# First half of the modulation's weights in four loads of every fourth partition, 48 KB a row

## Chip, cores, metric

One core of one Trainium2 chip. The metric is the device time of one execution in microseconds; lower is better.

Terms: SP is the engine whose queue issues nearly all loads here. A load is dealt to 16 DMA engines; each of its rows (the bytes that go to one partition) is one packet of the trace. PE is the matmul engine, DVE the vector engine; PE's granted clock is the share of its full clock that the chip let it have. "Stride" below means the step over partitions.

## The reference, cut to what matters

A decode step of a transformer block for 8 sequences: a modulation computed from `c`, attention over an 8192-long cache, and a gated MLP.

```python
mod = (_silu(c) @ w_mod).reshape(c.shape[0], 6, 1, -1)     # w_mod: 1024 x 6144, bf16
sa, ca, ga, sb, cb, gb = ...                               # six parts of mod
h = _layernorm(x) * (1 + ca) + sa
x = x + ga * attention(h, k_cache, v_cache, wq, wo)        # caches: 134 MB
h = _layernorm(x) * (1 + cb) + sb
return x + gb * mlp(h, W_gate, W_up, W_down)
```

`w_mod` is 12.6 MB, the first thing that is loaded and the first weights that are used. All inputs together are 185.6 MB.

## The kernel before: the parts that matter

`arena` is a buffer of 128 partitions. `load` queues a load, `pump` issues queued loads in order as soon as nothing unread lies where they go. Each partition gets 8 rows of `w_mod`, 96 KB; the first four (24 * D elements, 48 KB) are the first half.

```python
        def load(key, src, n, lo):
            place[key] = lo
            stream.append((key, src, n, lo))
        # ... pump(): dst = arena[:, lo:lo + n]; P.op("sp", ... e.dma_start(dst, src) ...)
        wm_src = w_mod.rearrange("(p k) n -> p (k n)", k=KC)
        # ... cut
        load(("wm", 0), wm_src[:, 0:D], D, 0)                      # 2 KB a row
        load(("wm0", 0), wm_src[:, D:24 * D], 23 * D, D)           # 46 KB a row
        load(("wm", 1), wm_src[:, 24 * D:48 * D], 24 * D, 24 * D)  # 48 KB a row: the second half
        # ... wq, then k, k, v for each of 8 sequences, wo, W_gate, W_up, W_down
        head = stream[2:]
        del stream[2:]
        pump()
        # ... c and A_x: two loads of 32 rows of 512 B, issued on ACT's queue
        stream.extend(head)
        # ... the matmuls of the modulation (line 522), in two halves:
        for i in range(2):
            # ... 48 matmuls
            P.op("pe", fns, reads=[R("hT"), slot_r(place["wm", i], place["wm", i] + 24 * D)], writes=[bank(0, 3)])
        # ... at the end of the program
        start_loads_first(nc, 3)     # moves SP's first 3 loads ahead of the start barrier's wait
```

The small first load was there so that the engines would have something to do early.

Of the kernel before, what the change touches and what calls it, by code (L numbers as in the profile page):

```python
# [236 lines left out]
def start_loads_first(nc, n):  # L237

    block = nc.main_func.blocks[0]

    def where(ins, engine, opcode=None):
        return [i for i, x in enumerate(ins) if x.engine == engine and opcode in (None, x.opcode)]

    for engine, ahead, total in ((mybir.EngineType.SP, 2, n), (mybir.EngineType.Activation, 2, 2)):
        ins = list(block.instructions)
        at = where(ins, engine, "EventSemaphore")[0]
        first = [ins[i] for i in where(ins, engine) if i > at][:total]
        assert all(x.opcode == "DMACopy" and not x.sync_info.on_wait for x in first), [x.opcode for x in first]
        names = {x.name for x in first}
        rest = [x for x in ins if x.name not in names]  # L250
        at = where(rest, engine, "EventSemaphore")[0]
        rest = rest[:at] + first[ahead:] + rest[at:]
        at = where(rest, engine)[0]
        block.instructions = rest[:at] + first[:ahead] + rest[at:]


def hold_weights(nc, held):

    names = {x.ins.name for x in held}
    for block in nc.main_func.blocks:  # L260
        block.instructions = [copy.replace(x, ldweights=False) if x.name in names else x for x in list(block.instructions)]


def bass_adaLN_cond__gqa_block_cached__glu_gated_reglu__decode_kernel(nc, A_x, A_k_cache, A_v_cache, A_wq, A_wo, B_x, B_W_gate, B_W_up, B_W_down, c, w_mod, out):
    B, _, D = A_x.shape
# [27 lines left out]
    with ExitStack() as es:  # L293
        E = es.enter_context

        def sb(name, shape, dtype):
            return E(nc.sbuf_tensor(name, shape, dtype))
# [4 lines left out]
        arena = sb("arena", [128, RING], dt.bfloat16)  # L302
# [74 lines left out]
        def slot_r(lo, hi):  # L377
            return ("arena", lo, hi)
# [2 lines left out]

        stream, place = [], {}

        def load(key, src, n, lo):
            place[key] = lo
            stream.append((key, src, n, lo))

        def pump():
            while stream:
                key, src, n, lo = stream[0]  # L390
                if P.unread("arena", lo, lo + n):
                    return
                stream.pop(0)
                dst = arena[:, lo:lo + n]
                P.op("sp", lambda e, dst=dst, src=src: e.dma_start(dst, src), writes=[slot_r(lo, lo + n)], dma=True,  # L395
                     own=key[0] if key[0] in ("ka", "kb", "v") else None)
                if key[0] in ("ka", "kb", "v"):
                    P.held[key] = (lo, lo + n)

        wm_src = w_mod.rearrange("(p k) n -> p (k n)", k=KC)  # L400
# [2 lines left out]
        g_src = B_W_gate.rearrange("(p k) n -> p (k n)", k=KC)  # L403
        u_src = B_W_up.rearrange("(p k) n -> p (k n)", k=KC)
        d_src = B_W_down.rearrange("(p k) n -> p (k n)", k=KF)
        load(("wm", 0), wm_src[:, 0:D], D, 0)
        load(("wm0", 0), wm_src[:, D:24 * D], 23 * D, D)
        load(("wm", 1), wm_src[:, 24 * D:48 * D], 24 * D, 24 * D)
        wq_parts = [(0, 4), (4, 8)]
        for i, (r0, r1) in enumerate(wq_parts):  # L410
# [9 lines left out]
        wd_parts = [(0, 14), (14, 21), (21, 25), (25, 27), (27, 28)]  # L420
        for i, (r0, r1) in enumerate(wd_parts):
            load(("wd", i), d_src[:, r0 * D:r1 * D], (r1 - r0) * D, VPART + r0 * D)
        head = stream[2:]
        del stream[2:]
        pump()
        for t, src in enumerate((c.rearrange("b (j n) -> (b j) n", j=4), A_x.rearrange("b o (j n) -> (b o j) n", j=4))):
            P.op("act", lambda e, t=t, src=src: e.dma_start(cx[:, t, :], src), writes=[R("cx", t, t + 1)], dma=True)
        stream.extend(head)
        P.pump = pump
        pump()  # L430


# [106 lines left out]
        for i, (r0, r1) in enumerate(wq_parts):  # L539
            lo, hi = place["wq", i], place["wq", i] + (r1 - r0) * 4096  # L540
# [11 lines left out]
        for z in range(2):  # L552
            src = ps[:, 4 + z, :].rearrange("p (u x r) -> p u r x", u=J, r=2)
            dst = qs[:, 16 * z:16 * z + 16, :].rearrange("p (u r) x -> p u r x", r=2)
# [146 lines left out]
        for z in range(2):  # L701
# [6 lines left out]
            dst = orow[:, 4 * z:4 * z + 4, :].rearrange("p j d -> p (j d)")  # L708
# [46 lines left out]
        for nm, b0 in (("gate", 0), ("up", 2)):  # L755
            lo, hi = place[nm, 0], place[nm, 0] + KC * F
# [18 lines left out]
        for i, (r0, r1) in enumerate(wd_parts):  # L775
            lo, hi = place["wd", i], place["wd", i] + (r1 - r0) * D
# [35 lines left out]

        P.plan()
        P.emit(nc, dict(sp=nc.sync, act=nc.scalar, pool=nc.gpsimd, dve=nc.vector, pe=nc.tensor), sems)
        start_loads_first(nc, 3)
        hold_weights(nc, holding)


# [26 lines left out]
```

## Time and profile before

| | |
|---|---|
| time, three runs | 436.29 us median (436.08 to 436.56) |
| bytes moved | 185.74 MB in a span of 434.9 us |
| busy: load queue, PE, DVE | 99.0%, 60%, 57% |

The page of the profile. "DMA" gives the busy share of the 16 DMA engines in 40 slices of the span (9 is 90% or more), "GB/s" counts a packet in the slice in which it starts, and the last lines are the chain of work that ended last.

```profile
span 434.9 us, 4853 instructions
...
DMA  9999999989999999999999999999999999999996
GB/s 374 452 431 434 433 434 437 471 375 440 440 413 428 455 440 407 434 455 413 431 464 422 416 434 464 410 425 443 458 398 431 443 464 410 448 429 429 427 418 255
DMA packets 5526, 185.74 MB, mean 427 GB/s; under 512 B 720, under 2 KB 784, under 8 KB 1168
...
q1 hardware_dynamic: 5376, 185.61, 99.0%
...
## 4 chain that ended last, share of the span: by engine, by line
DMA 11%; PE 4%; DVE 1%; SPq 0%; issue 0%
```

The engines that move data are hardly idle between the first slice and the last, and no other engine is near that. Time can be gained only where the DMA engines run below their usual rate, and that is at the start. The timeline of the first 36 us: start, duration, engine, line, operation, and in brackets the idle time before it and what ended it.

```profile
0.00 1.44 SPq L395 DMA_DIRECT2D arena<-in_w_mod_dram  x3
...
1.42 0.20 POOL L437 MEMSET identf<- 128x128 f32 x1 [0.98 <-POOLq L830]
1.57 22.18 SPq L395 DMA_DIRECT2D arena<-in_A_wq_dram  x2
...
9.78 0.58 PE L455 MATMUL ps<-cx,rsel 32*128 32x512 bf16 x1 [9.78 <-DMA cx<-in_A_x_dram]
...
19.23 4.16 PE L522 MATMUL ps<-arena,hT 128*32 128x512 bf16 x48
...
31.54 4.82 PE L522 MATMUL ps<-arena,hT 128*32 128x512 bf16 x48 [8.15 <-DMA arena<-in_w_mod_dram]
```

PE has the first half's matmuls done at 23.4 us and then waits 8.15 us for the second half's bytes. The issue of loads, with KB and the time from issue to landing:

```profile
arena<-in_w_mod_dram SPq DMA_DIRECT2D x1, 6144.0 KB, 30.4
arena<-in_w_mod_dram SPq DMA_DIRECT2D x1, 5888.0 KB, 16.5
arena<-in_w_mod_dram SPq DMA_DIRECT2D x1, 256.0 KB, 2.8
```

Below, "packet records" are the trace's list of packets: start, duration and size of each, without the engine or the partition. Time is counted from the start of SP's first issue.

### The profile page before, as it was taken

What the parts mean: (1) busy time and instruction counts of PE and PEld (TensorE: products, weight loads), DVE (VectorE), ACT (ScalarE), POOL (GpSimd) and SP (SyncE); (2) the same over time, 40 slices, a digit from 0 to 9 for tenths busy, and PEclk for the clock granted to TensorE, in tenths of its full rate; (3) what the DMA queues carried; (4) which work ended last, traced back from release to release, by engine and by line L of the source; (5) the groups of instructions that cost most, each with busy time, mean ns of one, the idle gap of its engine ahead of it and who ended that gap; (6) DMA issues with size and microseconds to landing.
All of it is one profiled execution on the core that took longest, in us unless ns stands there. A gap on an engine that the chain in (4) does not pass through costs nothing. (4 is left out here: it accounts for less than half of the span.)

```text
span 434.9 us, 4853 instructions
## 1 busy us (share of the span) xinstructions
PE 260.7 (60%) x2175; PEld 137.3 (32%) x2015; DVE 249.8 (57%) x345; ACT 29.8 (7%) x55; POOL 9.2 (2%) x24
## 2 busy tenths in 40 slices
PE   0325339566838874783977478487838856364247
PEld 0100003163218224421822352172226316241015
DVE  0603059747972985597299649739963974430021
ACT  1100010100020002002000200200020020100000
POOL 3000000000000000000000000000000000000000
PEclk9966569969978996998699599979968986885678
DMA  9999999989999999999999999999999999999996
GB/s 374 452 431 434 433 434 437 471 375 440 440 413 428 455 440 407 434 455 413 431 464 422 416 434 464 410 425 443 458 398 431 443 464 410 448 429 429 427 418 255
DMA packets 5526, 185.74 MB, mean 427 GB/s; under 512 B 720, under 2 KB 784, under 8 KB 1168
## 3 DMA queue, kind: packets, MB, share of 16 engines
q1 hardware_dynamic: 5376, 185.61, 99.0%
q8 instruction: 5, 0.08, 0.1%
q10 hardware_dynamic: 144, 0.04, 0.0%
q14 instruction: 1, 0.01, 0.0%
HBM read 185.63 MB, written 0.02 MB: 427 GB/s over the span
## 5 line engine op out<-in xcount | busy, mean ns | idle before, releaser
L584 DVE STREAM_TRANSPOSE kt<-arena 128x1024 uint32<-128x1024 uint32 x128 | 148.2, 1211 | 62.1 <-DVEq L181 44.7
L594 PE MATMUL ps<-kt,qpad 128*128 128x512 bf16 x512 | 133.9, 384 | 42.8 <-DVE kt L584 36.7
L634 PE MATMUL ps<-arena,pT 128*64 128x256 bf16 x1024 | 74.8, 321 | 51.0 <-PEq L181 51.0
L634 PEld LDWEIGHTS ps<-arena,pT 128*64 128x64 bf16 x1024 | 72.0, 132 | 53.2 <-issue 52.3
L594 PEld LDWEIGHTS ps<-kt,qpad 128*128 128x128 bf16 x512 | 40.5, 98 | 132.3 <-DVE kt L584 99.7
L624 DVE TENSOR_SCALAR pT<-pd,mqf 128x1024 bf16<-128x1024 bf16 x64 | 28.2, 503 | 0.6
L616 ACT ACTIVATE prb<-ps,bias 128x1024 bf16<-128x1024 f32 x16 | 17.7, 1110 | 138.8 <-DVE mjt L611 138.8
L622 DVE STREAM_TRANSPOSE pd<-prb 128x1024 bf16<-128x1024 bf16 x16 | 19.8, 1238 | 10.9 <-ACT prb L616 10.9
L600 DVE TENSOR_REDUCE negm<-ps 128x1 f32<-128x512 f32 x32 | 21.2, 661 | 4.5 <-PE ps L594 4.5
L762 PE MATMUL ps<-arena,hT 128*32 128x448 bf16 x128 | 10.7, 518 | 16.9 <-DMA arena<-in_B_W_up_dram 10.6
L769 DVE TENSOR_TENSOR kt<-ps,kt 128x448 bf16<-128x448 f32 x2 | 1.2, 620 | 27.8 <-PE ps L762 27.8
L546 PE MATMUL ps<-arena,hT 128*32 128x512 bf16 x64 | 7.2, 630 | 12.2 <-DMA arena<-in_A_wq_dram 12.2
L522 PE MATMUL ps<-arena,hT 128*32 128x512 bf16 x96 | 9.0, 551 | 8.2 <-DMA arena<-in_w_mod_dram 8.2
L653 ACT ACTIVATE oacc<-ps 128x32 f32 (+1 forms) x9 | 1.8, 198 | 158.6 <-PE ps L648 158.6
L575 POOL TENSOR_TENSOR qpad<-qR,mq 128x128 bf16<-128x128 bf16 x8 | 4.9, 607 | 310.7 <-DVE pT L624 258.2
L529 DVE COPY mod<-ps 128x512 f32<-128x512 f32 x2 | 1.3, 671 | 16.5 <-PE ps L522 16.5
L762 PEld LDWEIGHTS ps<-arena,hT 128*32 128x32 bf16 x64 | 2.3, 134 | 25.1 <-DMA arena<-in_B_W_up_dram 11.7
L557 DVE CAST kt<-ps 128x512 bf16<-128x512 f32 x1 | 0.7, 692 | 15.9 <-PE ps L546 15.9
L783 PE MATMUL ps<-arena,hmT 128*32 128x256 bf16 x84 | 6.4, 329 | 3.9 <-DMA arena<-in_B_W_down_dram 3.9
L606 PE MATMUL ps<-identf,negm 128*128 128x128 f32 x16 | 3.9, 326 | 7.8 <-DVE negm L604 7.8
L722 PE MATMUL ps<-arena,kt 128*32 128x256 bf16 x128 | 4.9, 328 | 4.6 <-DMA arena<-in_A_wo_dram 4.6
L546 PEld LDWEIGHTS ps<-arena,hT 128*32 128x32 bf16 x32 | 1.2, 137 | 18.2 <-DMA arena<-in_A_wq_dram 14.8
(99 smaller groups left out, 88.9 us busy)
## 6 DMA issues: line engine op xcount, KB each, us to landing
arena<-in_A_k_cache_dram SPq DMA_DIRECT2D x16, 4096.0 KB, 27.2
arena<-in_A_wq_dram SPq DMA_DIRECT2D x2, 4096.0 KB, 34.2
arena<-in_B_W_gate_dram SPq DMA_DIRECT2D x1, 7168.0 KB, 24.2
arena<-in_B_W_up_dram SPq DMA_DIRECT2D x1, 7168.0 KB, 28.8
arena<-in_w_mod_dram SPq DMA_DIRECT2D x1, 6144.0 KB, 30.4
arena<-in_w_mod_dram SPq DMA_DIRECT2D x1, 5888.0 KB, 16.5
arena<-in_B_W_down_dram SPq DMA_DIRECT2D x1, 3584.0 KB, 19.0
arena<-in_B_W_down_dram SPq DMA_DIRECT2D x1, 1792.0 KB, 22.9
```

The source lines that it names most:

```text
L522: fns.append(lambda e, w=w, pr=pr, j=j, kk=kk: hold(e.matmul(ps[32 * j:32 * j + 32, pr, :], hT[:, kk, :], w[:, 2 * pr:2 * pr + 2, j, :], s ...
L546: fns.append(lambda e, w=w, r=kk - r0, z=z, g=g, kk=kk: hold(e.matmul(ps[32 * g:32 * g + 32, 4 + z, :], hT[:, kk, :], w[:, r, g, z, :], st ...
L575: P.op("pool", lambda e: e.tensor_tensor(out=qpad[:, :, 24:152].rearrange("p u (q c) -> p u q c", q=4)[:, :, :, 0:J], in0=qR[:].rearrange( ...
L584: P.op("dve", lambda e_: e_.transpose(ktb[:, to:to + PART].bitcast(dt.uint32), arena[:, lo:lo + PART].bitcast(dt.uint32)), reads=[slot_r(l ...
L594: fns.append(lambda e_, t=t, r=r: e_.matmul(ps[:, e // 4, :].rearrange("p (c k) -> p c k", k=32), qpad[:, t * 2 + r, 24 - 8 * i:152 - 8 * ...
L600: P.op("dve", lambda e: e.tensor_reduce(negm[:, h:h + 1], ps[:, h, :], AX.X, ALU.max, negate=True), reads=[bank(h)] + (free(("ka", b)) if ...
L616: P.op("act", lambda e: e.activation(prb[:, f, :], ps[:, 2 * f:2 * f + 2, :].rearrange("p h n -> p (h n)"), ACT.Exp, bias=bias[:, 0:1], sc ...
L622: P.op("dve", lambda e: e.transpose(pd[:, f], prb[:, f]), reads=[R("prb", f, f + 1)], writes=[R("pd", 1024 * f, 1024 * f + 1024)])
L624: P.op("dve", lambda e, g=g: e.tensor_scalar(out=pT[:, f, :, :, g, :], in0=pd[:, f].rearrange("p (c i x) -> p c i x", c=32, i=2), scalar1= ...
L634: fns.append(lambda e, n=n, h=h, c_=c_, i=i, t=t: e.matmul(ps[64 * t:64 * t + 64, 5, 0:2 * Dh].rearrange("p (i d) -> p i d", d=Dh), pT[:, ...
L762: fns.append(lambda e, w=w, kk=kk, h=h, j=j, b0=b0: hold(e.matmul(ps[32 * j:32 * j + 32, b0 + h, 0:H], hT[:, kk, :], w[:, kk, j, h, :], st ...
L783: fns.append(lambda e, w=w, r=k - r0, k=k, i2=i2, j=j: e.matmul(ps[32 * j:32 * j + 32, 4, 0:256], hmT[:, k, 1 - i2:33 - i2], w[:, r, i2, j ...
```

## The change

Its intent: no small rows, full-length rows from the first microsecond. The first half comes in four loads, each of every fourth partition, so each load has 32 rows of 48 KB, two for each engine. Why not 32 neighbouring partitions? Because those lie on half of SBUF's ports.

```diff
-        def load(key, src, n, lo):
+        def load(key, src, n, lo, dst=None):
             place[key] = lo
-            stream.append((key, src, n, lo))
+            stream.append((key, src, n, lo, arena[:, lo:lo + n] if dst is None else dst))
@@ pump() takes dst from the queue: cut @@
-        load(("wm", 0), wm_src[:, 0:D], D, 0)
-        load(("wm0", 0), wm_src[:, D:24 * D], 23 * D, D)
+        place["wm", 0] = 0
+        for i in range(4):
+            load(("wm0", i), wm_src[i::4, 0:24 * D], 6 * D, 6 * D * i, arena[i:128:4, 0:24 * D])
         load(("wm", 1), wm_src[:, 24 * D:48 * D], 24 * D, 24 * D)
@@ cut @@
-        head = stream[2:]
-        del stream[2:]
+        head = stream[4:]
+        del stream[4:]
@@ cut @@
-        start_loads_first(nc, 3)
+        start_loads_first(nc, 5)
```

More of the change, by code (lines that the diff above doesn't have):

```diff
@@ L382, in bass_adaLN_cond__gqa_block_cached__glu_gated_reglu__decode_kernel @@
         stream, place = [], {}
-        def load(key, src, n, lo):
+        def load(key, src, n, lo, dst=None):
             place[key] = lo
-            stream.append((key, src, n, lo))
+            stream.append((key, src, n, lo, arena[:, lo:lo + n] if dst is None else dst))
         def pump():
             while stream:
-                key, src, n, lo = stream[0]
+                key, src, n, lo, dst = stream[0]
                 if P.unread("arena", lo, lo + n):
@@ L393, in pump @@
                 stream.pop(0)
-                dst = arena[:, lo:lo + n]
                 P.op("sp", lambda e, dst=dst, src=src: e.dma_start(dst, src), writes=[slot_r(lo, lo + n)], dma=True,
```

## The prediction

> **What bounds the kernel now.** The DMA engines. The page's 40 slices show them at nine tenths or more nearly throughout; the queue table gives the load queue 99.0% of 16 engines' span, 427 GB/s over 434.9 us. The chain of waits ends with the loads of W_gate and W_down and 4 us of arithmetic behind the last bytes. PE is busy 60%, DVE 57%: neither sets the time. The change can only give what it takes out of slow DMA time.
>
> **Where the start loses time.** In the trace's packet records (time from the first load's issue) the first 2 KB row starts at 1.01 us, and all 16 engines have started by 1.39. Each moves eight 2 KB rows (84 ns at best, up to 556 here) and starts its first 46 KB row between 1.77 and 2.46 us. From 1 to 2 us the engines move 229 GB/s, from 2 to 4 us 384, afterwards 430 to 434: about 0.7 us lost. A 46 KB row takes 1740 ns, a 48 KB row 1815, both 27 B/ns.
>
> **The change.** It removes 128 rows of 2 KB and 128 of 46 KB, and adds four loads of 32 rows of 48 KB: two rows an engine and load. Bytes are the same. Packets should fall from 5526 to about 5430, those under 8 KB from 1168 to about 1072.
>
> *Gain.* An engine's 48 KB rows should begin where its 2 KB rows began, 1.01 to 1.39 us, and take 8 x 1.815 = 14.5 us, plus up to 0.45 us for a slow first row (some first 46 KB rows took 2.19 us) and 0.15 for small packets. The second half of the weights, which now starts at 16.2 to 16.7 us, should start near 15.8 to 16.3: a gain of 0.3 to 0.6 us. Since DMA is the limit to the end, it arrives there whole.
>
> *Off the path.* SP issues two loads more before the start barrier, 0.33 to 0.42 us each: POOL's memset of identf moves from 1.42 to about 2.1 us. The small loads of c and x slip between whole rows; with no 2 KB rows ahead, the first small matmul (L455, 9.75 us) starts near 12 to 13 us, the first modulation matmul (L522) near 22 instead of 19.2. It takes 4.2 us and must end before the second half lands, near 31: it will.
>
> **The risk.** The Trainium skill, "DMA: Bandwidth & Descriptors", section "The descriptor swizzle", says that a load of 128 partitions gives each engine the eight partitions of one SBUF port; the trace agrees in so far as all 16 run at full rate side by side. The section covers that shape only. With every fourth partition each port holds two of the 32 rows, but if rows are dealt to engines in plain order, two engines write one port at a time. The first 6.3 MB would then run at half rate: rows near 3.6 us, the second half starting near 29 us, the end 13 us later, near 449. I give this about one chance in five; nothing in the trace of before decides it.
>
> **Prediction.** 436.0 us; range 435.2 to 449.0, wide because of the second case. Faster by over 2%: 0.01; within 2%: 0.78; slower: 0.21.
>
> **What would show it.** Right: 48 KB packets of about 1.8 us from the first microsecond on, second half near 16 us, later GB/s and tail unchanged. Wrong: first rows well over 2 us, GB/s near 220 in the first 30 us, PE's wait at L522 13 us later. Also wrong if a late x (after 20 us) made the first modulation matmul the limit, or if later loads were issued so late that the queue ran dry.

## More of the kernel before

Executions come in two states. Most of this kernel's take 436 to 437 us; some take 444 to 446 us, of the kernel before as well as of changed ones.

## The result, and the profile after

| | before | after |
|---|---|---|
| median of 6 runs, us | 436.30 (435.88 to 444.27) | 436.91 (436.34 to 445.25) |
| ratio of fast runs | 1 | 1.0012, 95% interval 0.9999 to 1.0026 |

A ratio is the mean time of one kernel's fast runs over the mean of the other's of the same rounds, so it is not quite the ratio of the medians.

The profiled run of the changed kernel fell into the slow state (445.25 us). These are its stretches, with busy time of PE, PEld, DVE, ACT and POOL, then PE's granted clock, DMA share and GB/s:

```profile
0.00:8.00 8.00, 0.00 (x0) 0.00 (x0) 0.00 (x0) 1.28 (x1) 4.29 (x16) 1.00 0.99 390
8.00:80.00 72.00, 27.43 (x201) 7.24 (x105) 22.53 (x40) 4.58 (x7) 0.46 (x1) 0.72 1.00 387
90.00:160.00 70.00, 47.49 (x375) 28.00 (x372) 47.68 (x66) 5.00 (x10) 1.27 (x2) 0.88 1.01 435
```

From 8 to 80 us the engines are as busy as ever but move 387 GB/s instead of 435. The kernel before has such runs too (444 to 445 us), so this is no effect of the change, and this profile is not used further. The profile after, from here on, is that of the same kernel run again (run `after_again`). Its page, the lines that answer to those shown of before:

```profile
span 435.3 us, 4856 instructions
...
DMA  9999999999999999999999999999999999999995
GB/s 364 434 449 434 432 434 440 464 393 467 413 422 434 470 410 422 434 470 394 434 449 458 394 431 452 428 425 461 422 425 434 473 404 464 392 423 444 435 407 242
DMA packets 5430, 185.74 MB, mean 427 GB/s; under 512 B 752, under 2 KB 816, under 8 KB 1072
...
q1 hardware_dynamic: 5280, 185.61, 98.8%
...
## 4 chain that ended last, share of the span: by engine, by line
DMA 13%; DVE 5%; PE 5%; issue 0%; DVEq 0%
```

The packet counts are those predicted (5430, and 1072 under 8 KB). The busy share is no better. The timeline:

```profile
0.00 3.41 SPq L394 DMA_DIRECT2D arena<-in_w_mod_dram  x5
...
1.85 0.20 POOL L437 MEMSET identf<- 128x128 f32 x1 [1.42 <-POOLq L830]
3.55 22.07 SPq L394 DMA_DIRECT2D arena<-in_A_wq_dram  x2
...
10.72 0.58 PE L455 MATMUL ps<-cx,rsel 32*128 32x512 bf16 x1 [10.72 <-DMA cx<-in_A_x_dram]
...
20.17 5.08 PE L522 MATMUL ps<-arena,hT 128*32 128x512 bf16 x48
...
32.16 4.21 PE L522 MATMUL ps<-arena,hT 128*32 128x512 bf16 x48 [6.92 <-DMA arena<-in_w_mod_dram]
```

The second half's matmuls, which wait for bytes in both kernels, start at 32.16 us instead of 31.54 (31.66 in two more profiles of before, 32.31 in another of the change). The change made the start of the stream later, not earlier. And SP took 3.41 us for five issues where it took 1.44 for three. The four loads land 11.1 us after their issue (median):

```profile
arena<-in_w_mod_dram SPq DMA_DIRECT2D x4, 1536.0 KB, 11.1
arena<-in_w_mod_dram SPq DMA_DIRECT2D x1, 6144.0 KB, 29.3
```

In the packet records, rows after an engine's first take 1815 ns in the median, the full rate. So the case that the prediction feared, two engines on one port, did not come about. But the first row starts at 1.32 us instead of 1.01, and the 16 first rows take 2.38 to 2.83 us, 2.54 on average.

Theories for the lost time:

1. Loads at a stride of four partitions are issued and dealt out later.
2. Long first rows start slowly, whatever load they belong to: either because the issue of the following loads gets in their way (2a), or by themselves (2b).
3. The number of issues in the first 3 us slows the start.

### The profile page after: what moved, and what is told of

It reads as the page before. It is cut to its first block, busy times and chain, and to the rows that moved or that the text cites. A ratio compares the mean times of both kernels' runs of the same rounds, so it can differ in the third digit from the quotient of the medians.

```text
span 443.9 us, 4856 instructions
## 1 busy us (share of the span) xinstructions
PE 264.6 (60%) x2175; PEld 139.7 (31%) x2015; DVE 249.7 (56%) x345; ACT 29.8 (7%) x55; POOL 9.2 (2%) x24
## 2 busy tenths in 40 slices
DMA packets 5430, 185.74 MB, mean 418 GB/s; under 512 B 752, under 2 KB 816, under 8 KB 1072
## 5 line engine op out<-in xcount | busy, mean ns | idle before, releaser
L762 PE MATMUL ps<-arena,hT 128*32 128x448 bf16 x128 | 12.1, 572 | 14.5 <-DMA arena<-in_B_W_up_dram 10.9
L722 PE MATMUL ps<-arena,kt 128*32 128x256 bf16 x128 | 6.4, 393 | 4.8 <-DMA arena<-in_A_wo_dram 4.8
L546 PEld LDWEIGHTS ps<-arena,hT 128*32 128x32 bf16 x32 | 1.2, 137 | 20.8 <-DMA arena<-in_A_wq_dram 17.4
```

Of the source, the lines that this page charges most:

```text
L546: fns.append(lambda e, w=w, r=kk - r0, z=z, g=g, kk=kk: hold(e.matmul(ps[32 * g:32 * g + 32, 4 + z, :], hT[:, kk, :], w[:, r, g, z, :], st ...
L722: fns.append(lambda e, w=w, k=k, j=j: e.matmul(ps[32 * j:32 * j + 32, 5, 0:256], oX[:, k, :], w[:, k, j, :], start=(k == 0), stop=(k == KO ...
L762: fns.append(lambda e, w=w, kk=kk, h=h, j=j, b0=b0: hold(e.matmul(ps[32 * j:32 * j + 32, b0 + h, 0:H], hT[:, kk, :], w[:, kk, j, h, :], st ...
```

## Experiments

Two measures are used. The first is the ratio of times; it resolves about 0.13%, 0.6 us. The second is read from the packet records and resolves more: the time by which 6.3 MB have been moved (the first half of the weights), and its parts. A packet's bytes are spread evenly over its duration for this. "Idle" is the time in the first 8 us in which an engine has no packet in flight, the mean of 16 engines. "Excess" is what the packets that start in the first 6 us take beyond the usual time of their size (1815 ns for 48 KB, 1740 for 46 KB, 84 for 2 KB; between sizes seen later, interpolated), over 16.

| run | SP's first issue, us | first row starts, us | idle, us | excess, us | 6.3 MB moved, us |
|---|---|---|---|---|---|
| before (three profiles) | 0.39 | 1.01, 1.01, 1.02 | 1.15, 1.16, 1.07 | 0.50, 0.54, 0.70 | 16.33, 16.36, 16.43 |
| the change (two fast profiles) | 0.54, 0.55 | 1.32, 1.33 | 1.42, 1.43 | 0.74, 0.84 | 16.75, 16.86 |
| one_long | 0.39 | 1.01 | 1.29 | 0.61 | 16.53 |
| four_cols | 0.39 | 1.01 | 1.15 | 0.64 | 16.52 |
| two_strided | 0.55 | 1.32 | 1.54 | 0.66 | 16.78 |
| small_then_strided | 0.39 | 1.02 | 1.23 | 0.74 | 16.65 |
| first_8k | 0.39 | 1.01 | 1.11 | 0.63 | 16.45 |
| first_512b | 0.39 | 1.02 | 1.43 | 0.90 | 17.09 |
| four_blocks | 0.39 | 1.01 | 1.17 | 3.86 | 31.50 |

Three profiles of before differ by 0.10 us in the last column, two of the change by 0.11; a difference of 0.1 between single profiles says nothing. All kernels gave correct results. Diffs are against the changed kernel unless said otherwise; the number in `stream[...]` and in `start_loads_first` follows the number of loads and is left out.

### after_again: the change once more

No edit.

> The changed kernel again, for a profile in the fast state. Both theories: 436.5 to 437.0 us. Theory 1 (loads of 32 rows at a stride are issued and dealt out later) and theory 2 (long first rows start slowly whatever the load's shape) both expect the profile to repeat what the slow one had in its first 4 us: SP takes 0.47 to 0.59 us for each of the four issues (0.33 to 0.42 before), the first row starts near 1.3 us and the last engine's near 2.4 us, first rows take 2.2 to 2.8 us, later rows 1.815; second half of the weights starts at 16.8 to 17.4 us (16.2 to 16.7 before).

Measured: ratio 1.0002 (0.9987 to 1.0017), median 436.77 us over all six runs, two of them slow. SP's issues of the four loads took 0.47 to 0.59 us, the first row started at 1.32 us, the last of the engines' first rows at 1.73 (not 2.4), first rows took 2.38 to 2.83 us, and the second half started at 16.6 to 17.3 us. The start is as in the slow profile, but for the last engine. In time the loss does not stand out from the noise: 1.0012, 1.0002.

### one_long: long rows without the stride

```diff
-        for i in range(4):
-            load(("wm0", i), wm_src[i::4, 0:24 * D], 6 * D, 6 * D * i, arena[i:128:4, 0:24 * D])
+        load(("wm0", 0), wm_src[:, 0:24 * D], 24 * D, 0)
```

> First half in one load of 128 rows of 48 KB: the long rows alone, without the 32-row loads and without the 2 KB rows. Theory 1: SP's first issue 0.39 us, engines start at 1.0 to 1.4 us, second half starts at 15.8 to 16.3 us, total 435.7 to 436.1 (0.3 to 0.6 under before). Theory 2: engines start at 1.0 to 1.4 us but first rows take over 2.2 us, second half starts at or after 16.5 us, total 436.3 to 436.9.

Measured: ratio 1.0000 (0.9987 to 1.0013). The issue took 0.39 us and the first row started at 1.01 us, as theory 1 has it. But the 16 first rows took 1.81 to 2.90 us, 2.42 on average, the second half started at 16.3 to 17.4 us, and 6.3 MB were moved at 16.53 us: 0.1 to 0.2 us later than before, 0.2 to 0.3 earlier than in the change. That fits theory 2 for part of the loss and theory 1 for the rest (one profile; see the split below). The prediction's gain fails here too, and here there is no stride to blame: full rows from the first microsecond do not start faster than 2 KB rows.

### four_cols: as many issues, full loads

```diff
-            load(("wm0", i), wm_src[i::4, 0:24 * D], 6 * D, 6 * D * i, arena[i:128:4, 0:24 * D])
+            load(("wm0", i), wm_src[:, 6 * D * i:6 * D * (i + 1)], 6 * D, 6 * D * i)
```

> First half in four loads of all 128 rows, 12 KB a row: as many issues as in the change, but full loads. Theory 1: issues 0.33 to 0.42 us, starts at 1.0 to 1.4 us, total as one_long within 0.2 us (435.7 to 436.2). If it is the number of issues in the first 3 us that slows the start (theory 3): starts or first rows as late as in the change, total 436.5 to 437.

Measured: ratio 1.0000 (0.9987 to 1.0013). First row at 1.01 us, 6.3 MB at 16.52 us, as in one_long. SP needed 2.60 us for its five issues and lost nothing by it. Theory 3 falls.

### four_blocks: neighbouring partitions

```diff
-            load(("wm0", i), wm_src[i::4, 0:24 * D], 6 * D, 6 * D * i, arena[i:128:4, 0:24 * D])
+            load(("wm0", i), wm_src[32 * i:32 * i + 32, 0:24 * D], 6 * D, 6 * D * i,
+                 arena[32 * i:32 * i + 32, 0:24 * D])
```

> First half in four loads of 32 neighbouring partitions each, 48 KB a row. The risk named in the prediction, made on purpose: 32 neighbouring partitions lie on 8 of 16 SBUF ports by the skill's map. If two engines then share a port, rows take near 3.6 us instead of 1.815, the second half starts at 29 to 31 us and the total is 448 to 451 us. If engines fall out of step and take turns with the ports, or the port is no limit, 437 to 440.

("The skill's map" is the table of ports cited below.)

Measured: 451.82 us, ratio 1.0352 (1.0337 to 1.0367), a little past the range expected. Rows of the first half took 3.84 us in the median (1.815 in the change), and the second half started at 30.9 to 32.4 us. Its first stretches:

```profile
0.00:16.00 16.00, 0.00 (x0) 0.00 (x0) 0.00 (x0) 1.28 (x1) 4.28 (x16) 1.00 0.97 201
16.00:31.00 15.00, 1.75 (x5) 1.10 (x5) 7.22 (x19) 1.90 (x3) 0.00 (x0) 1.00 1.01 210
31.00:46.00 15.00, 5.31 (x48) 0.68 (x16) 0.00 (x0) 0.00 (x0) 0.00 (x0) 0.87 0.99 416
```

The last two columns are DMA share and GB/s: engines busy all the time, at half the bytes. This is what a limit of the ports would do. The Trainium skill, "SBUF — State Buffer", section "Door 1: The DMA port swizzle", lists for partitions 0 to 31 eight of 16 ports and an asymptote of about 218 GB/s; the packet records show 219 GB/s from 1.6 to 4 us. That makes the ports the likely cause, but not the only one possible: the 32 source rows are neighbours in DRAM too (3.1 MB, where the change's are spread over 12.6 MB), and no run separates the two. Either way the step of four in the change is worth 15 us against the obvious way to cut a load in four. The run also shows that SP's longer first issue belongs to the step and not to the number of rows: 32 neighbouring rows were issued in 0.39 us.

### before_again: what the comparison resolves

No edit of the kernel before.

> The kernel before against itself: what the comparison can resolve, and a second profile of it. Expected ratio 1.000 with an interval of about 0.13% either way. In the first profile of before the engines lost 0.4 us between 50 and 100 us that the other kernels' profiles did not lose. If that is chance, this profile has packets at their usual times there, and the lead of 0.42 us over the changed kernel at 6.3 MB is still there at 185 MB (DMA end near 431.4 us); if it belongs to the kernel, it comes back here (DMA end near 431.85).

Measured: the kernel before against itself, 0.9992 (0.9979 to 1.0005). One run of before in these rounds took 665.57 us, unexplained and left out as slow. In the second profile 185.4 MB were moved at 429.91 us; in the first it was 430.28, because packets between 50 and 100 us took longer there. No fast profile since showed as much of that, so I take it for chance. (The expectation's "DMA end" is the last byte of the loads. It came at 431.73 us, against 431.85 in the first profile and 432.25 in after_again, so the 431.4 expected for chance was not met. The 185.4 MB mark was chosen afterwards; by either measure the change is behind.)

### quiet_start: nothing else issued

one_long, with c, x and all later loads held back until a memset on POOL is done:

```diff
+            P.op("act", lambda e, t=t, src=src: e.dma_start(cx[:, t, :], src), reads=[R("hm4")], ...)  # c and x, moved down
+                     reads=[R("hm4")] if key == ("wm", 1) else [],                                     # SP's second load
@@ start_loads_first: SP's first load alone is moved ahead, none of ACT's @@
```

> one_long, with every other load (c, x and all of SP's) held back until POOL's memset of hm4, near 5 us, so that the first load's rows run alone. Theory 2a (issuing and dealing out the following loads slows the first rows): first rows take 1.815 us as later ones, 6.3 MB are moved at 15.6 to 15.9 us (16.53 in one_long). Theory 2b (the first rows are slow by themselves, a cold start of the 16 engines' reads): first rows still take 2.2 to 2.9 us, 6.3 MB at 16.4 to 16.7 us. Total 436.0 to 437 us either way, unless x, which comes some 4 us later, holds up the modulation's matmuls beyond 31 us.

Measured: ratio 1.0005 (0.9991 to 1.0019). The next issue came at 4.6 us. The 16 first rows still took 1.81 to 2.94 us, 2.55 on average, with no other load in flight, and 3 MB were moved at 8.91 us (8.85 in one_long). 2a falls. Of the two, 2b is left: first rows are slow with no other load issued. Whether the dealing out of the load's own later rows slows them was not tested. Nor is it each engine's first row that is slow: the engine that starts last takes the usual 1.81 us for it, from 1.89 us here and from 2.69 us in one_long, while those that start before 1.2 us take 2.3 to 2.9. So the slow time looks like one of the start of the stream and not of each engine. The profile fell into the slow state from about 11 us on, so its 6.3 MB mark is not used.

### first_8k and first_512b: how long should the first rows be?

The kernel before with its 2 KB rows replaced:

```diff
-        load(("wm", 0), wm_src[:, 0:D], D, 0)
-        load(("wm0", 0), wm_src[:, D:24 * D], 23 * D, D)
+        load(("wm0", 0), wm_src[:, 0:4 * D], 4 * D, 0)               # first_8k;   first_512b: 0:256
+        load(("wm0", 1), wm_src[:, 4 * D:24 * D], 20 * D, 4 * D)     #             256:24 * D
```

> The kernel before with first rows of 8 KB instead of 2 KB, then 40 KB. If the loss of the first 4 us is nearly the same whatever the rows are (theory 2b), 6.3 MB are moved at 16.3 to 16.6 us (16.33 before, 16.52 with 12 KB, 16.53 with 48 KB) and the total is within 0.13% of before. If longer first rows avoid the 2 KB rows' extra cost, as the prediction had it, 15.9 to 16.2 us.

> The kernel before with first rows of 512 B instead of 2 KB. By the series so far (6.3 MB at 16.53 us with 48 KB, 16.52 with four times 12 KB, 16.45 with 8 KB, 16.34 with 2 KB) shorter first rows lose less; if that goes on, 16.2 to 16.3 us. If the cold start costs the same whatever is read first, and the rest of the series is the spread of the engines, 16.3 to 16.5. The total can't tell: within 0.15% of before.

Measured: first_8k 1.0009 (0.9995 to 1.0023), 6.3 MB at 16.45 us, like before within what single profiles tell. first_512b 1.0008 (0.9992 to 1.0025), 6.3 MB at 17.09 us: outside both expectations, the series turns round. From 1.2 to 2.4 us only 9.7 to 14.4 of the 16 engines had a packet in flight (means of stretches of 0.4 us). The eight 512 B rows are done before the next load's rows are there, and those, the first long ones, are slow again (2.61 us on average for rows of 47.5 KB). A first load that is too short costs more than one that is too long.

### two_strided: the stride with more rows

```diff
-        for i in range(4):
-            load(("wm0", i), wm_src[i::4, 0:24 * D], 6 * D, 6 * D * i, arena[i:128:4, 0:24 * D])
+        for i in range(2):
+            load(("wm0", i), wm_src[i::2, 0:24 * D], 12 * D, 12 * D * i, arena[i:128:2, 0:24 * D])
```

> First half in two loads of every second partition, 64 rows of 48 KB each. If it is the step over partitions that makes SP's issue long (0.54 us at step 4; 0.39 with 32 neighbouring rows), these issues take 0.5 us or more and the first row starts near 1.3 us; if it is the small number of rows, 0.39 us and 1.0 us. Rows after the first at 1.815 us, no sharing of ports. Total 436.3 to 437.0.

Measured: ratio 1.0016 (1.0000 to 1.0032), unclear. Issues of 0.55 and 0.58 us, first row at 1.32 us, later rows at 1815 ns, 6.3 MB at 16.78 us: the change's numbers. With four_blocks (32 rows, no step, 0.39 us) this says that the step makes the issue long and the start late, not the number of rows. (The step is in the source rows as well as in the partitions; these were not separated.)

### small_then_strided: the stride behind a normal first load

```diff
+        load(("wm0", 0), wm_src[:, 0:D], D, 0)
         for i in range(4):
-            load(("wm0", i), wm_src[i::4, 0:24 * D], 6 * D, 6 * D * i, arena[i:128:4, 0:24 * D])
+            lo, n = D + 5888 * i, 5888
+            load(("wm0", 1 + i), wm_src[i::4, D:24 * D], n, lo, arena[i:128:4, D:24 * D])
```

> The 2 KB load of before first, then the other 46 KB of each row in four loads of every fourth partition. If the change loses at the first issue (0.54 us instead of 0.39, first row at 1.32 instead of 1.01 us) and in its slow long first rows, and nothing later, this kernel is as good as before: first row at 1.0 us, 6.3 MB moved at 16.3 to 16.5 us (16.33 and 16.36 in before, 16.75 in the change), though its strided loads are issued at 0.5 to 0.6 us each. If strided loads lose elsewhere too, 16.6 us or more.

Measured: ratio 1.0009 (0.9992 to 1.0026). First row at 1.02 us, but 6.3 MB at 16.65 us, not 16.3 to 16.5. So the first issue is not all that a stride costs. The four issues took 0.52, 0.47, 0.80 and 0.60 us, and the first 46 KB rows took 2.16 us on average, against 1.93 to 1.95 in the profiles of before. Why they are slower was not found.

### before_third and after_third: repeats

No edits.

> A third profile of the kernel before. 6.3 MB at 16.3 to 16.4 us; 185.4 MB at 429.9 us, as in the second profile, if the lost 0.4 us of the first profile were chance.

> Another profile of the changed kernel. First row at 1.32 us, 6.3 MB at 16.7 to 16.8 us, 185.4 MB at 430.3 us: the 0.42 us lost in the first 5 us arrive at the end.

Measured (one run each; their packets took the usual times): before 16.43 us and 430.01 us for the two marks, the change 16.86 and 430.44 us. With before_again and after_again (429.91 and 430.33; those two ran on different chips, the third profiles on one): the change is 0.39 and 0.43 us late at 6.3 MB in the two pairs, and 0.42 and 0.43 us late at 185.4 MB. What is lost at the start arrives whole at the end of the loads.

It need not arrive at the end of the kernel. before_third's one profiled run took 436.98 us although its loads were on time. The last stretch of before_again, busy time of PE first, granted clock third from the end:

```profile
424.00:436.00 12.00, 6.74 (x140) 5.33 (x134) 1.39 (x4) 0.00 (x0) 0.00 (x0) 0.98 0.53 219
```

The same stretch of before_third:

```profile
424.00:436.00 12.00, 9.28 (x142) 6.83 (x138) 1.39 (x4) 0.00 (x0) 0.00 (x0) 0.77 0.54 223
```

The matmuls of W_down's first 21 rows and the issue of the outputs, from the timeline of before_again:

```profile
423.52 3.24 PE L783 MATMUL ps<-arena,hmT 128*32 128x256 bf16 x56 [3.61 <-DMA arena<-in_B_W_down_dram]
427.76 1.71 PE L783 MATMUL ps<-arena,hmT 128*32 128x256 bf16 x28 [1.01 <-DMA arena<-in_B_W_down_dram]
...
433.12 0.36 SPq L809 DMA_DIRECT2D out_dram<-ob  x1
```

And from that of before_third:

```profile
423.52 7.68 PE L783 MATMUL ps<-arena,hmT 128*32 128x256 bf16 x84 [3.23 <-DMA arena<-in_B_W_down_dram]
...
434.02 0.36 SPq L809 DMA_DIRECT2D out_dram<-ob  x1
```

At a granted clock of 0.98 over the last 12 us these 84 matmuls need 4.95 us (273 ns each in the median) and PE waits for bytes in between; at 0.77 (0.50 from 423.5 to 427 us) they need 7.68 us (418 ns each) and PE itself is last. The outputs leave 0.9 us later, with the loads on time. That is twice the change's effect, and one way in which the times of single runs come to scatter more than the loads do.

## Why the prediction was right or wrong

The class (same) and the range (435.2 to 449.0) held: 436.91 us. That is no credit to the reasoning: the range was wide because of a case that did not come about, and any effect under 2% is "same". The direction of the small effect was wrong by the packet records; the times do not resolve it.

- **What bounds the kernel: right, with one correction.** The loads carry a delay of the first microseconds to their end unchanged (0.39 and 0.43 us at 6.3 MB, 0.42 and 0.43 us at 185.4 MB). But "it arrives there whole" is true of the loads only; behind them PE at a low granted clock can be last.
- **The gain: wrong.** The step that failed is "An engine's 48 KB rows should begin where its 2 KB rows began, 1.01 to 1.39 us, and take 8 x 1.815 = 14.5 us, plus up to 0.45 us for a slow first row". They began at 1.32 to 1.73 us, because SP's issue of a load with a stride takes 0.54 us instead of 0.39 and the first row follows 0.78 us after it instead of 0.62. And the first row was 0.73 us slow on average (2.54 against 1.815), 0.83 in the other profile. Measured sum: idle 1.42 against 1.07 to 1.16 us, excess 0.74 to 0.84 against 0.50 to 0.70. A forecast of 0.3 to 0.6 us gained became some 0.4 us lost at both marks.
- **The reading behind it: wrong.** I put the 0.7 us lost in the first 4 us down to the 2 KB rows. one_long and quiet_start show that the loss is there with 48 KB rows as well; a loss of about that size is there whatever rows of 2 KB or more come first, and short rows merely showed it in their durations. (After 4 us the rate was not at once "430 to 434" either: the records give 418 GB/s from 4 to 6 us.)
- **The risk: sized well, and not met.** Of the case of two engines on one port the prediction said 449 us; four_blocks, which was built to make it, took 451.8. The change itself ran at full rate after the first rows. How the rows are dealt to engines is not recorded; that all of them run at 1815 ns side by side suggests that no two shared a port for long.
- **Off the path: right in kind, too large.** POOL's memset moved from 1.42 to 1.85 us (predicted 2.1), the first small matmul from 9.78 to 10.72 (predicted 12 to 13), the first modulation matmuls from 19.23 to 20.17 (predicted 22). They still ended, at 25.3 us, well before the second half landed.
- **Packets: right**, 5430 and 1072.

Of the change's 0.4 us, about 0.1 to 0.2 us goes with long first rows (one_long against before) and 0.2 to 0.3 us with the stride (the change against one_long). The parts are as large as a few profiles' scatter, so their split is rough; that the stride costs is shown by two_strided and small_then_strided as well; the 0.1 to 0.2 us of the long rows rest on one profile each of one_long and four_cols and are not shown by repeats. At 185.4 MB these stood at 430.18 and 430.05 us, against 429.91 and 430.01 in the later profiles of before: four_cols was all but level there. The times alone (1.0012 and 1.0002, each within about 0.14%) could not have shown either. No version here beat the kernel before: its 2 KB first rows gave the earliest 6.3 MB of all sizes tried, though 8 KB can't be told from it.

What stays open: why long rows that start in the first microsecond of the stream take 0.6 to 0.8 us more on average than later ones, and why a stride makes issue and start longer.

## What to carry to other kernels

When a load must be cut by partitions, take every n-th partition (2 and 4 were tried) and not a block: at n = 4 both have 32 rows, but the block ran at half rate and cost 15 us. Do not put a load with a stride first: its issue took 0.15 us longer here and its first row started 0.3 us later. A slow start is not proof that the rows in it are too short; try longer rows before building on it, and read the effect from the time by which a given number of bytes has moved, because a total that ends behind a throttled PE does not resolve half a microsecond.

## What the Trainium skill lacked or had wrong

- "SBUF — State Buffer", section 'Can I just issue two DMAs to hit both halves?', says "The only way to hit all 16 ports is one transfer spanning all 128 partitions." Loads of 32 rows at every fourth partition, and of 64 rows at every second, ran at the full rate here: 1815 ns a row of 48 KB on 16 engines, as with 128 rows. The sentence holds if "spanning" means the range and not the number of partitions; the page should say so.
- "DMA: Bandwidth & Descriptors", section "The descriptor swizzle", describes loads of 128 partitions only; for other shapes it points to how the number of engines is chosen, and that does not say which rows go to which engine. Here 32 rows at a step of four: full rate; 32 neighbours: 3.84 us a row instead of 1.815.
- "DMA: Bandwidth & Descriptors", section "Latency and other measured facts", gives about 600 ns to the first byte for loads issued on SP, without saying from when. Here the first packet starts 0.62 us after the end of SP's issue (1.01 less 0.39), which agrees; with a step over partitions it is 0.78 us (1.32 less 0.54), and the issue itself takes 0.54 us instead of 0.39. No page has the cost of the step.
- No page has the slow start: the first 48 KB rows take 2.4 to 2.65 us on average over the 16 engines instead of 1.815, even with no other load issued (2.55), though one that starts late takes 1.81.
- No page has the slow runs: in the slow profile of the change, for some 70 us, rows of 48 KB take 2036 ns instead of 1815 and then rows of 32 KB 1359 instead of 1213 (387 GB/s instead of 435), a run takes 444 to 445 us, and PE's granted clock over the whole run (0.834 against 0.835) doesn't show it.
